# Sparse attention and a two-layer network on one core: scores ahead of values in the opening, a longer lead of the second layer, and uneven rounds of first-layer units

## The chip, the core and the metric

The kernel runs on one core of a Trainium2 chip. A core has four compute engines: TensorE (PE: matrix products, with its weight loads PEld beside them), VectorE (DVE), ScalarE (ACT) and GpSimd (POOL), and SyncE (SP), which here only issues DMAs. Each engine takes its instructions in the order of the program, and engines wait for one another through semaphores. The DMAs of the kernel are issued from SP and from POOL. PE writes its products to PSUM, which has eight banks of 128 x 512 fp32. The metric is the time of the program on the device in microseconds (us).

## What is computed

The reference is an attention with a sparse mask, and a two-layer network with a cosine gate behind it. There are 8 batches and 8 heads, a sequence of 576 and a head width of 64, hence 4608 tokens of width 512.

```python
mask = np.abs(pos[:, None] - pos[None, :]) <= 32          # a band
mask = mask | is_global[:, None] | is_global[None, :]     # and 8 global positions
scores = np.where(mask, q @ k.T / 8.0, -1e9)
attn = softmax(scores)
x = (attn @ v)            # heads side by side: 4608 x 512
h = x @ w_in              # 512 -> 2048
g = h * np.cos(h)
out = g @ w_out           # 2048 -> 512
```

## The kernel before

**Attention** goes by pairs of heads, 32 pairs in all (four to a batch). A pair takes these steps:

- `k`, `q` (local_k, local_q): bring K and Q into the layout of the scores. For pairs 0 to 9 PE turns them into a bank of tag h, and ACT copies them out (L604, L615, L616). From pair 10 on they come ready turned by DMA, and DVE copies them (L607, L619).
- `s` (scores): products of K and Q into three banks of tag s and a fourth (tag o in the opening, tag h later); then ACT's exponentials (L634 and L638, from pair 10 on L702 and L707) and DVE's products with the mask (L635 and L639, later L703 and L708).
- `p` (values): products with V into the tile pv, of which there is one (L646, later L719); then DVE's sums, reciprocals and the normalised rows xn (L660 to L666, later L724 to L730).
- `x` (turn_x): PE turns xn (L678, later L744) through a bank of tag s, and DVE copies it into xT, the input of the first layer. At the end of a batch POOL copies the columns of the global tokens (L687, L752).
- `n` (x_squares): ACT's squares of xn (L818), for a check of the value range.

**The network** goes by 9 tiles of 512 tokens. A first-layer unit, written `1`, is one of 16 groups of 128 hidden columns: four matmuls into a bank of tag h (L762), then ACT's cosine (L768) and DVE's product g (L769), which frees the bank. Tag h has two banks, taken in turn. Only between the marks `+` and `-` does every second pair of units take tag s instead. A second-layer unit, written `2`, is a quarter of an output tile of 128 tokens: four matmuls (L800). Four units fill a tile, which is copied out by DVE (L807) where its number within the 512 tokens is even and by ACT (L805) where it is odd, and goes to DRAM by an SP DMA (L809). Such a tile takes the one bank of tag o; odd ones take tag s in the tail and between `+` and `-`.

**The order is written by hand.** The program is emitted as the strings say, step by step, and each engine runs its share in that order.

- FRONT (L56) is the opening, pairs 0 to 9. Beside the steps above it has `L` (loads of K and Q), `M` (a DVE memset and the loads of V of the next half batch, `vn`), `C` (POOL's cast of it), `y` (value_rows: the V rows of the global tokens, PE at L409 and ACT at L410), `E` and `Y` (gathers of global rows by POOL), `H` (their casts and turning), `g` (global columns of K and Q by POOL), `W` and `O` (loads of the two weights), `K` (casts of K, Q and V to fp16 in DRAM), `f` (fillers: matmuls of ones into an unused part of pv, L493), and `m` and `t` (the matmuls of a first-layer unit, and its ACT and DVE part, apart).
- Rounds 4 to 15 follow, one for each two pairs (`a` and `z` are the round's two pairs, `c` and `d` the next round's). Round 4 is MID: pairs 8 and 9 are done in FRONT, so MID is first-layer and second-layer units while the data of pair 10 arrive. Round 5 is FIFTH, round 6 SIXTH, and rounds 7 to 15 are ORDER.
- Then comes the tail: the loop from L1042 on, `one()` and `two()` in turn, with squares of the weights on ACT (L826), their sums on DVE (L828), and four times weight_norms: a matmul with ones into a tile pn (L833) and a maximum on DVE (L834).

A `1` or `2` that cannot run yet is left out. `one()` needs its tokens ready (ready[0] grows by one 512-token tile after every odd round). `two()` needs the g that it reads to have been issued, and, ahead of the tail, fewer than outs_by[0] second-layer units done so far, which is 8 for each round from round 4 on.

Of the kernel before, what the change touches and what calls it, by code (L numbers as in the profile page):

```python
# [9 lines left out]
FP32 = mybir.dt.float32  # L10
# [9 lines left out]
P = 128  # L20
# [3 lines left out]
G = 8  # L24
# [20 lines left out]
TT = 512  # L45
NTT = NT // TT

ORDER = "sa 2 2 2 2 sz pa 1 1 2 xa pz G 1 1 2 xz n 1 1 2 kc qc 1 kd qd 2 1"

MID = ("+ 1 1 1 1 Z0 1 1 1 Z1 1 1 Z2 1 1 A0 n1 1 Z3 1 1 1 Z4 1 1 A1 n2 1 1 1 Z5 A2 1 1 1 n3 B5 1 2 2 g10 g11 kc qc V10 K6 2 2 1 1 2 2 kd qd - 2 2")  # L50

FIFTH = "sa G 2 2 2 2 sz pa 1 1 2 xa U10 K7 pz 2 2 2 kc qc xz n kd qd"

SIXTH = "sa 2 2 2 2 sz pa 1 1 2 xa pz G 1 1 2 xz n 1 1 D0 2 kc qc D1 1 kd qd D2 2 1"

FRONT = ("M1 s0 E0 C0 E1 L2 k1 q1 w4 y0.0 s1 f4 C1 H0 p0 M2 Y0 L3 y0.1 k2 q2 f6 x0 p1 y1.0 s2 k3 q3 f6 x1 M3 H1 C2 p2 g4 g5 g6 "  # L56
         "y1.1 s3 g7 I k4 q4 f6 x2 M4 p3 y2.0 s4 C3 L4 W0 k5 q5 f6 x3 p4 y2.1 s5 g8 g9 W1 W2 W3 k6 q6 f6 x4 p5 y3.0 s6 C4 k7 q7 f6 n0 x5 p6 "
         "y3.1 s7 k8 q8 f6 x6 p7 y4.0 s8 H2 k9 q9 f6 x7 p8 y4.1 s9 O m m x8 K5 p9 t t + m m t t x9 -")
WARM = 13
OK_ALL = float(P * (B * NP * 2 * BP + B))  # L60

# [143 lines left out]
def kernel(  # L205
# [18 lines left out]
    ps = es.enter_context(tc.tile_pool(name="ps", bufs=2, space=PSUM))  # L224
# [96 lines left out]
    p8 = keep.tile([P, 1], FP32)  # L321
# [432 lines left out]
    def mlp_in(t, f):  # L754
        if f == 0:
            g_of[t] = work.tile([P, NF, TT], FP16, tag="g", name="g")
        g16 = g_of[t]
        tag = "s" if spare[0] and f % 4 > 1 else "h"
        ph = ps.tile([P, TT], FP32, tag=tag, bufs={"s": 3, "h": 2}[tag], name="ph")
        ph_of.append((ph, g16[:, f]))  # L760
        for j in range(NC):
            nc.tensor.matmul(ph, w_in16[:, j, f * P : (f + 1) * P], xT[:, j, t * TT : (t + 1) * TT],  # L762
                             start=(j == 0), stop=(j == NC - 1))

    def mlp_act():
        ph, g = ph_of.pop(0)
        cos = work.tile([P, TT], FP16, tag="cos", bufs=3)
        nc.scalar.activation(cos, ph, AF.Sin, bias=pio2)  # L768
        nc.vector.tensor_tensor(g, cos, ph, ALU.mult)  # L769
# [20 lines left out]
    def mlp_out(t, u):  # L790
        g16 = g_of[t]
        s, part = u // 4, u % 4
        if part == 0:
            tag = "s" if (tail[0] or spare[0]) and s % 2 else "o"
            po_of[t] = ps.tile([P, DM], FP32, tag=tag, bufs={"s": 3, "o": 1}[tag], name="po")
        po = po_of[t]
        if t == NTT - 1 and s == 3:
            return last_out(g16, po, part)
        for f in range(4 * part, 4 * part + 4):
            nc.tensor.matmul(po, g16[:, f, s * P : (s + 1) * P], w_out16[:, f],  # L800
                             start=(f == 0), stop=(f == NF - 1))
        if part == 3:
            o = work.tile([P, DM], FP32, tag="osb", bufs=3)
            if s % 2:
                nc.scalar.copy(o, po)  # L805
            else:
                nc.vector.tensor_copy(o, po)  # L807
            r0 = t * TT + s * P
            nc.sync.dma_start(out[r0 : r0 + P, :], o)  # L809
# [4 lines left out]
    def x_squares(s):  # L814

        xn = xn_of.pop(s)
        n = P * (NK5 if s < HY else BP)
        nc.scalar.activation(view(xn, (BP * P, 2), (1, n)), view(xn, (BP * P, 2), (1, n)), AF.Square,  # L818
                             accum_out=x_sq[:, s : s + 1])
# [3 lines left out]
    def weight_squares(c, j):  # L823
        if j == 0:
            w_sq[c] = work.tile([P, NC, 512], FP16, tag="wsq", bufs=1, name="wsq")
        nc.scalar.activation(w_sq[c][:, j], w_in16[:, j, c * 512 : (c + 1) * 512], AF.Square)  # L826
        if j:
            nc.vector.tensor_tensor(w_sq[c][:, 0], w_sq[c][:, 0], w_sq[c][:, j], ALU.add)  # L828

    def weight_norms(c):  # L830
        sq = w_sq.pop(c)
        pn = ps.tile([P, 512], FP32, tag="h", bufs=2)
        nc.tensor.matmul(pn, ones16, sq[:, 0], start=True, stop=True)  # L833
        nc.vector.tensor_reduce(wmax4[:, c : c + 1], pn, AX.X, ALU.max)  # L834

# [22 lines left out]
    def raise_flag(count):  # L858
        tot, onesf = count
        pt = ps.tile([P, 512], FP32, tag="h", bufs=2)  # L860
        nc.tensor.matmul(pt[0:1, 0:1], tot, onesf, start=True, stop=True)
        okf = work.tile([1, 1], FP32, tag="okf", bufs=1)
        nc.vector.tensor_scalar(okf, pt[0:1, 0:1], OK_ALL, None, ALU.is_equal)
        nc.vector.tensor_copy(ok_flag, okf)
# [4 lines left out]
    def one(act=True):  # L869
        for _ in range(1):  # L870

            if ins_q and ins_q[0][0] < ready[0] and ins_q[0][0] < outs_q[0][0] + 2:
                t, f = ins_q.pop(0)
                mlp_in(t, f)
                if act:
                    mlp_act()
                ready[1] = t * NF + f + 1

    def two(n=1):
        for _ in range(n):  # L880
            t, u = outs_q[0] if outs_q else (NTT, 0)

            need = min(t * NF + 4 * (u % 4) + 7, (t + 1) * NF)
            if outs_q and need <= ready[1] and (tail[0] or NTT * NF - len(outs_q) < outs_by[0]):
                mlp_out(*outs_q.pop(0))

    outs_by = [0]
# [12 lines left out]
    with tc.manual_schedule():  # L900
# [73 lines left out]
        def casts(s):  # L974

            for pr in (2 * s + 2, 2 * s + 3):
                if pr < B * NP:
                    globals_kq(pr)
            if 5 < s < 2 * B - 2:
                nc.gpsimd.tensor_copy(gate, xn_of[s][0:1, 1, 0, 0:1])  # L980
                cast_half(s + 2, "vkq")
# [5 lines left out]
        def bring(s):  # L987

            turn_half(s)
            load_values(2 * s)  # L990
            load_values(2 * s + 1)
# [8 lines left out]
        ready[0] = 1  # L1000
        for step in FRONT.split():
            if step in "+-":
# [3 lines left out]
            f(*[int(x) for x in (step[1:] or "0").split(".")])  # L1006
        ready[0], front[0] = 2, False
        for s in range(4, B * NP // 2):
            outs_by[0] = 8 * (s - 3)
            for step in {4: MID, 5: FIFTH, 6: SIXTH}.get(s, ORDER).split():  # L1010
                if step == "1":
                    one()
                elif step == "m":
                    one(False)
                elif step == "t":
                    mlp_act()
                elif step in "+-":
                    spare[0] = step == "+"
                elif step == "2":
                    two()  # L1020
                elif step == "n":
                    x_squares(s - 1)
                elif step == "R":
                    ready[0] = 2
                elif step == "T":
                    bring(s + 2)
                elif step == "G":
                    casts(s)
                elif step[0] in "cvWCOVABDNU" or step[1].isdigit():
                    (STEPS | OTHER)[step[0]](*[int(x) for x in (step[1:] or "0").split(".")])  # L1030
                else:
                    f, pr = (STEPS | OTHER)[step[0]], 2 * s + "azcd".index(step[1])
                    if pr < B * NP:
                        f(pr, *[int(x) for x in step[2:]])
            if s % 2 == 1:
                ready[0] = s // 2 + 1 + (s // 2 == B - 1)
            if 3 < s < B * NP // 2 - 2:
                bring(s + 2)
# [2 lines left out]
        tail[0] = True  # L1041
        for i in range(NTT * NF):  # L1042
            one()
            two()
            if i % 5 < 4 and i < 20:
                weight_squares(i // 5, i % 5)
            elif i < 20:
                weight_norms(i // 5)
            if i == 22:
                count = finish_check()  # L1050
            if i == 34:
                raise_flag(count)
# [36 lines left out]
```

## Time and profile before

| | us |
|---|---|
| median of 3 runs | 357.35 (356.35 to 358.64) |
| the profiled execution | 355.8 |
| its span, first to last instruction | 354.1 |
| PE busy in the span | 334.3 |
| start of the long run of first-layer units (end of the opening) | 59.82 |
| one round (the scores of `sa`, at 155.56, to the next, at 172.70) | 17.14 |
| last 128 x 256 copy of the output begins | 348.42 |

A row of a timeline is start, length, engine, line, operation, output and inputs, shape, and how many instructions are merged in it; in brackets stands how long the engine was idle before it and what ended that wait. The lengths of matmuls are modelled and overlap (a 128 x 512 matmul is shown as 379 ns, but four of them follow one another in 0.86 us), so starts say more than lengths.

### The profile page before, as it was taken

What the parts mean: (1) busy time and instruction counts of PE and PEld (TensorE: products, weight loads), DVE (VectorE), ACT (ScalarE), POOL (GpSimd) and SP (SyncE); (2) the same over time, 40 slices, a digit from 0 to 9 for tenths busy, and PEclk for the clock granted to TensorE, in tenths of its full rate; (3) what the DMA queues carried; (4) which work ended last, traced back from release to release, by engine and by line L of the source; (5) the groups of instructions that cost most, each with busy time, mean ns of one, the idle gap of its engine ahead of it and who ended that gap; (6) DMA issues with size and microseconds to landing.
All of it is one profiled execution on the core that took longest, in us unless ns stands there. A gap on an engine that the chain in (4) does not pass through costs nothing.

```text
span 354.1 us, 8454 instructions
## 1 busy us (share of the span) xinstructions
PE 334.3 (94%) x3203; PEld 172.8 (49%) x3203; DVE 250.2 (71%) x611; ACT 245.3 (69%) x423; POOL 107.0 (30%) x221
## 2 busy tenths in 40 slices
PE   7879889999989999999999999999999999999993
PEld 2567665444445454545454444444444444444442
DVE  6567778987588697869787878787877556556410
ACT  8767898895666878777787877777686865644300
POOL 8773918333161507041623253233002000000000
PEclk9998999999999999999999999999999999999999
DMA  5999895999999999999999999999970001000111
GB/s 85 180 170 159 136 200 84 203 158 115 175 155 171 151 191 136 175 139 170 149 186 134 151 145 198 157 163 170 110 118 1 31 36 53 32 30 30 58 62 68
DMA packets 165891, 44.58 MB, mean 126 GB/s; under 512 B 153764, under 2 KB 160996, under 8 KB 165668
## 3 DMA queue, kind: packets, MB, share of 16 engines
q1 hardware_dynamic: 105860, 26.70, 52.3%
q0 software_dynamic: 59984, 17.28, 48.8%
q8 instruction: 27, 0.44, 0.5%
q14 instruction: 20, 0.16, 0.2%
HBM read 44.41 MB, written 19.17 MB: 180 GB/s over the span
## 4 chain that ended last, share of the span: by engine, by line
PE 73%; ACT 10%; DVE 6%; issue 5%; DMA 3%; SPq 1%; POOL 0%; ACTq 0%; POOLq 0%; DVEq 0%
PE po L800 32%; PE ph L762 30%; PE st L699 2%; PE tx L744 2%; DVE g L769 2%; ACT e L702 2%; ACT e L634 2%; PE pv L646 2%; ACT cos L768 2%; DMA vn<-in_v_dram 2%; ACT e L638 1%; ACT e L707 1%; PE pv L719 1%; DMA gidx_col<-in_global_idx_dram 1%; PE po L782 1%
## 5 line engine op out<-in xcount | busy, mean ns | idle before, releaser
L762 PE MATMUL ph<-xT,w_in 128*128 128x512 f16 x576 | 140.5, 379 | 2.8 <-DVE g L769 2.0
L768 ACT ACTIVATE cos<-ph,pio 128x512 f16<-128x512 f32 x144 | 96.8, 686 | 60.9 <-PE ph L762 58.5
L800 PE MATMUL po<-w_out,g 128*128 128x512 f16 x560 | 135.4, 379 | 0.0
L769 DVE TENSOR_TENSOR g<-cos,ph 128x512 f16<-128x512 f16 x144 | 95.7, 684 | 44.6 <-ACT cos L768 43.8
L762 PEld LDWEIGHTS <-w_in 128*128 128x128 f16 x576 | 54.2, 97 | 67.4 <-issue 7.9
L800 PEld LDWEIGHTS <-g 128*128 128x128 f16 x560 | 53.7, 98 | 63.6
L703 DVE TENSOR_TENSOR pm<-e,mask 128x512 f16<-128x512 f16 x44 | 18.7, 426 | 18.8 <-ACT e L702 17.4
L702 ACT ACTIVATE e<-st 128x512 f16<-128x512 f32 x44 | 23.9, 595 | 10.1 <-PE st L699 10.0
L980 POOL COPY gate<-xn 1x1 f16<-1x1 f16 x8 | 1.4, 179 | 85.8 <-DVE xn L730 85.8
L752 POOL COPY xT<-xg 128x4 f16 x48 | 15.6, 325 | 32.6 <-DVE xT L747 29.9
L272 POOL DMA_DIRECT2D q<-in_q_dram x11 | 23.9, 2176 | 0.0
L818 ACT ACTIVATE xn<-xn 128x1536 f16<-128x1536 f16 (+1 forms) x16 | 22.5, 1408 | 0.0
L730 DVE TENSOR_TENSOR xn<-pv,r_all 128x768 f16<-128x768 f32 x22 | 21.1, 958 | 1.0
L805 ACT COPY o<-po 128x512 f32<-128x512 f32 x17 | 9.9, 585 | 14.7 <-PE po L800 14.5
L807 DVE COPY o<-po 128x512 f32<-128x512 f32 x18 | 12.4, 690 | 9.2 <-PE po L800 8.6
L272 POOL DMA_DIRECT2D k<-in_k_dram x11 | 18.1, 1642 | 1.2 <-issue 1.2
L646 PE MATMUL pv<-vw,pm 128*128 128x65 f16 (+2 forms) x200 | 13.0, 203 | 3.3 <-DVE pm L639 3.3
L768 ACT ACT_TABLE_LOAD x12 | 15.4, 1283 | 0.2
L607 DVE COPY kw<-kT 128x1320 f16<-128x1320 f16 x22 | 15.4, 699 | 0.0
L702 ACT ACT_TABLE_LOAD x11 | 14.1, 1283 | 0.2
L699 PEld LDWEIGHTS <-kw 64*128 64x128 f16 x484 | 8.5, 95 | 10.8 <-issue 8.1
L699 PE MATMUL st<-qb,kw 64*128 64x64 f16 x484 | 11.3, 191 | 1.5 <-DVE qb L619 1.1
(185 smaller groups left out, 386.6 us busy)
## 6 DMA issues: line engine op xcount, KB each, us to landing
out_dram<-o SPq DMA_DIRECT2D x35, 256.0 KB
vw<-v SPq DMA_DIRECT2D x32, 165.0 KB
v<-in_v_dram POOLq DMA_DIRECT2D x11, 288.0 KB, 5.2
k<-in_k_dram POOLq DMA_DIRECT2D x11, 288.0 KB, 7.1
q<-in_q_dram POOLq DMA_DIRECT2D x11, 288.0 KB, 14.5
vn<-in_v_dram SPq DMA_DIRECT2D x20, 120.0 KB
w_in<-in_moe_w_in_dram POOLq DMA_DIRECT2D x4, 512.0 KB
w_out<-in_moe_w_out_dram POOLq DMA_DIRECT2D x1, 2048.0 KB
```

The costliest lines, as they stand in the source:

```text
L272: nc.gpsimd.dma_start(dst[s].rearrange("t (h d) -> t h d", h=4), dview(src, base, (D, S), (S * D, 4), (1, D)))
L646: nc.tensor.matmul(pv[p0 : p0 + m, h, X * slot : X * slot + X], pm[:, h * CN + OFF[t] + c0 : h * CN + OFF[t] + c0 + m], vp[:, t, h0 + h], ...
L699: nc.tensor.matmul(st[j // 8 * 2 + h][:, j % 8 * C : j % 8 * C + C], kp[hp, j], qp[hp, j], start=True, stop=True)
L702: nc.scalar.activation(e[:, 0:512], st[h], AF.Exp, scale=scale)
L703: nc.vector.tensor_tensor(view(pm[:, h], (1, 512)), e[:, 0:512], view(mask, (1, 512)), ALU.mult)
L730: nc.vector.tensor_tensor(view(xn, (384, 2), (D, 6), (1, D)), view(pv, (512, 2), (65, 6), (1, D)), view(rp, (6, 2), (1, 6), (0, D)), ALU.mult)
L752: nc.gpsimd.tensor_copy(xT[:, :, bass.ds(pool_idx[g] + b * S, 1)], xg[:, :, g : g + 1])
L762: nc.tensor.matmul(ph, w_in16[:, j, f * P : (f + 1) * P], xT[:, j, t * TT : (t + 1) * TT], start=(j == 0), stop=(j == NC - 1))
L768: nc.scalar.activation(cos, ph, AF.Sin, bias=pio2)
L769: nc.vector.tensor_tensor(g, cos, ph, ALU.mult)
L800: nc.tensor.matmul(po, g16[:, f, s * P : (s + 1) * P], w_out16[:, f], start=(f == 0), stop=(f == NF - 1))
L818: nc.scalar.activation(view(xn, (BP * P, 2), (1, n)), view(xn, (BP * P, 2), (1, n)), AF.Square, accum_out=x_sq[:, s : s + 1])
```

## The change

Four things are changed.

1. **FRONT.** The scores of the next pair now stand ahead of the values of this one (`s1 y0.0 f4 k2 q2 .. p0 .. s2`, `.. x0 p1 .. s3`, where it was `s1 f4 .. p0 .. x0 p1 .. s2`). The fillers fall from 52 to 18, the late gathers of V (`Y0`) move from ahead of `L3` to behind `C4`, `L4` moves ahead of `I`, and three `g` move ahead of `C2`.
2. **The lead of the second layer.** outs_by is 4 higher from round 4 on, and MID has four more `2`, so 12 units are done in round 4 for 8. All later rounds do 8 as before, each one output tile further on: the four units behind `sa` are now the odd tile, and the four that are spread over the rest of the round the even one. The tail has 44 second-layer units left where it had 48.
3. **Uneven rounds.** Even rounds have ten first-layer units (SIXTH too) and odd rounds six, where all had eight. Three of them then stand in a row in odd rounds behind `pz G`, and in even rounds from 8 on behind `xz n`. In the tail four steps of the loop do two first-layer units.
4. **weight_norms** takes its tile from tag s (three banks), not from tag h.

```diff
-ORDER = "sa 2 2 2 2 sz pa 1 1 2 xa pz G 1 1 2 xz n 1 1 2 kc qc 1 kd qd 2 1"
+EVEN = "sa 2 2 2 2 sz pa 1 1 2 xa pz G 1 1 2 xz n 1 1 1 2 kc qc 1 1 kd qd 2 1"
+ODD = "sa 2 2 2 2 sz pa 1 1 2 xa pz G 1 1 1 xz n 1 2 kc qc 2 kd qd 2"

-MID = ("+ 1 1 1 1 Z0 1 1 1 Z1 1 1 Z2 1 1 A0 n1 1 Z3 1 1 1 Z4 1 1 A1 n2 1 1 1 Z5 A2 1 1 1 n3 B5 1 2 2 g10 g11 kc qc V10 K6 2 2 1 1 2 2 kd qd - 2 2")
+MID = ("+ 1 1 1 1 Z0 1 1 1 Z1 1 1 Z2 1 1 A0 n1 1 Z3 1 1 1 Z4 1 1 A1 n2 1 1 1 Z5 A2 1 1 1 n3 B5 1 2 2 g10 g11 kc qc V10 K6 2 2 1 1 2 2 2 2 kd qd 2 2 - 2 2")
 FIFTH = "sa G 2 2 2 2 sz pa 1 1 2 xa U10 K7 pz 2 2 2 kc qc xz n kd qd"
-SIXTH = "sa 2 2 2 2 sz pa 1 1 2 xa pz G 1 1 2 xz n 1 1 D0 2 kc qc D1 1 kd qd D2 2 1"
+SIXTH = "sa 2 2 2 2 sz pa 1 1 2 xa pz G 1 1 2 xz n 1 1 D0 2 kc qc D1 1 1 kd qd D2 2 1 1"

-FRONT = ("M1 s0 E0 C0 E1 L2 k1 q1 w4 y0.0 s1 f4 C1 H0 p0 M2 Y0 L3 y0.1 k2 q2 f6 x0 p1 y1.0 s2 k3 q3 f6 x1 M3 H1 C2 p2 g4 g5 g6 "
-         "y1.1 s3 g7 I k4 q4 f6 x2 M4 p3 y2.0 s4 C3 L4 W0 k5 q5 f6 x3 p4 y2.1 s5 g8 g9 W1 W2 W3 k6 q6 f6 x4 p5 y3.0 s6 C4 k7 q7 f6 n0 x5 p6 "
-         "y3.1 s7 k8 q8 f6 x6 p7 y4.0 s8 H2 k9 q9 f6 x7 p8 y4.1 s9 O m m x8 K5 p9 t t + m m t t x9 -")
+FRONT = ("M1 s0 E0 C0 E1 L2 k1 q1 w4 s1 y0.0 f4 k2 q2 C1 H0 p0 M2 L3 y0.1 s2 k3 q3 f2 x0 p1 M3 H1 g4 g5 g6 C2 y1.0 s3 g7 L4 I k4 q4 f2 x1 p2 M4 y1.1 s4 "
+         "C3 W0 k5 q5 f2 x2 p3 y2.0 s5 g8 g9 W1 W2 W3 k6 q6 f2 x3 p4 y2.1 s6 C4 Y0 k7 q7 f2 x4 p5 n0 y3.0 s7 k8 q8 f2 x5 p6 y3.1 s8 H2 k9 q9 f2 x6 p7 y4.0 s9 "
+         "x7 p8 y4.1 O m m x8 K5 p9 t t + m m t t x9 -")
...
     def weight_norms(c):
-        pn = ps.tile([P, 512], FP32, tag="h", bufs=2)
+        pn = ps.tile([P, 512], FP32, tag="s", bufs=3)
...
         for s in range(4, B * NP // 2):
-            outs_by[0] = 8 * (s - 3)
-            for step in {4: MID, 5: FIFTH, 6: SIXTH}.get(s, ORDER).split():
+            outs_by[0] = 8 * (s - 3) + 4
+            for step in {4: MID, 5: FIFTH, 6: SIXTH}.get(s, ODD if s % 2 else EVEN).split():
...
         for i in range(NTT * NF):
             one()
+            if 12 < i < 17:
+                one()
             two()
```

## The prediction

> **What bounds the kernel now.** I read the page's table of busy time first, then busy time by stretches, then who waited for whom on TensorE (PE), then the timeline of one round, of the tail and of the opening.
>
> ```profile
> span 354.1 us, 8454 instructions
> PE 334.3 (94%) x3203; PEld 172.8 (49%) x3203; DVE 250.2 (71%) x611; ACT 245.3 (69%) x423; POOL 107.0 (30%) x221
> ```
>
> PE is the engine to watch, but 94% is a mean over stages. By stretches (PE busy is the first number after the length, then PEld, DVE, ACT, POOL, the granted clock, DMA):
>
> ```profile
> 10.00:28.00 18.00, 14.67 (x336) 11.62 (x334) 10.24 (x38) 11.97 (x31) 13.46 (x16) 0.94 1.11 172
> 28.30:53.80 25.50, 21.98 (x469) 17.71 (x468) 19.35 (x61) 22.12 (x50) 11.58 (x34) 0.98 1.00 166
> 59.80:121.00 61.20, 59.20 (x444) 27.86 (x441) 48.75 (x113) 44.05 (x74) 24.59 (x43) 1.00 1.40 161
> 121.00:276.00 155.00, 154.33 (x1481) 75.81 (x1480) 124.09 (x277) 117.86 (x190) 43.13 (x98) 1.00 1.35 145
> 276.00:314.00 38.00, 36.24 (x166) 16.03 (x164) 22.19 (x40) 24.60 (x41) 0.00 (x0) 1.00 0.10 36
> ```
>
> From 121 to 276 us (the rounds, ORDER) PE is busy 154.33 of 155.00: there is no wait to win there, and any wait that the change makes is added in full, since PE takes its work in order and has no slack to swallow it. Time can be won in the opening (before 60 us, PE idle for 6.9 us of the first two stretches) and in the tail (1.8 us idle of 38). The named waits of PE, first from 276 us on, then between 60 and 121:
>
> ```profile
> PE ph L762 <- DVE g L769: 1.7, 4, 0.4
> ```
> ```profile
> PE st L699 <- DVE qb L619: 1.1, 1, 1.1
> ```
>
> **The rounds.** This is the largest term, so it comes first. A first-layer unit (`1`) needs one of the two banks of tag h, which is free again when VectorE (DVE) has written g of the unit two allocations before. One round, PE, then ScalarE (ACT), then DVE (start, length, instruction):
>
> ```profile
> 155.56 0.49 PE L699 MATMUL st<-qb,kw 64*128 64x64 f16 x22
> ...
> 164.35 1.90 PE L762 MATMUL ph<-xT,w_in 128*128 128x512 f16 x8
> 166.09 1.03 PE L800 MATMUL po<-w_out,g 128*128 128x512 f16 x4
> 166.95 0.50 PE L744 MATMUL tx<-ident,xn 128*128 128x128 f16 x6
> 167.43 1.89 PE L762 MATMUL ph<-xT,w_in 128*128 128x512 f16 x8
> 169.15 1.03 PE L800 MATMUL po<-w_out,g 128*128 128x512 f16 x4
> 170.01 1.03 PE L762 MATMUL ph<-xT,w_in 128*128 128x512 f16 x4
> 172.70 0.49 PE L699 MATMUL st<-qb,kw 64*128 64x64 f16 x22
> ```
> ```profile
> 159.98 1.08 ACT L702 ACTIVATE e<-st 128x512 f16<-128x512 f32 x2 [0.79 <-PE st L699]
> 166.87 1.47 ACT L818 ACTIVATE xn<-xn 128x1536 f16<-128x1536 f16 x1
> 168.49 0.69 ACT L768 ACTIVATE cos<-ph,pio 128x512 f16<-128x512 f32 x1
> ```
> ```profile
> 159.65 0.69 DVE L807 COPY o<-po 128x512 f32<-128x512 f32 x1
> 166.70 1.27 DVE L769 TENSOR_TENSOR g<-cos,ph 128x512 f16<-128x512 f16 x2
> 169.21 0.69 DVE L769 TENSOR_TENSOR g<-cos,ph 128x512 f16<-128x512 f16 x1 [0.73 <-ACT cos L768]
> 172.40 0.53 DVE L607 COPY kw<-kT 128x1320 f16<-128x1320 f16 x1
> 172.85 0.46 DVE L619 COPY qb<-qT 128x616 f16<-128x616 f16 x1
> ```
>
> Before, the units after `pz` stand as `1 1 2 xz n 1 1 2`. The third starts at 167.43, and the g that frees its bank ends at about 166.70 + 0.68 = 167.38: just in time, because `2` and `xz` (166.09 to 167.43) stand between.
>
> Odd round: `1 1 1 xz n 1`. The third unit is due at 166.09 and waits for the same g until 167.38: 1.3 us. Behind it stand `xz`, the last unit and three output units, and the whole rest of the round shifts. Then the end: the squares of `n` (with cos behind them: 168.49 - 166.87 = 1.6) now stand between the cos of the third and of the last unit. The third unit ends at 167.4 + 0.86 (a unit: half of 169.15 - 167.43) = 168.25; its cos (0.2 to begin, 0.69 long) ends at about 169.1, the squares at 170.7, the last cos at 171.3, its g at 172.0, the copies kw and qb (0.53 + 0.46, a little overlapped) at 172.9. PE wants the next scores at 168.25 + 0.48 (xz) + 4 x 0.86 = 172.2: 0.7 us more. And the output tile that ends the round is now an even one, whose copy is DVE's (before, an odd one, ACT's) and stands behind the second pair's kw and qb: 172.9 + 0.9 + 0.69 = 174.5, while the one bank of tag o is wanted behind the scores (0.45), at 173.35: 1.15 us.
>
> In all rounds the four output units behind `sa` now end an odd tile, whose copy goes to ACT:
>
> ```profile
> L805 ACT COPY o<-po 128x512 f32<-128x512 f32 x17 | 9.9, 585 | 14.7 <-PE po L800 14.5
> ```
>
> It falls between the two heads' pairs of exponentials, in a gap of 0.79 that ends at 159.98; begun at 159.65, as DVE's copy was, it ends at 160.24, so those exponentials and all behind them come 0.3 later. DVE's 0.69 at 159.65 falls away in a place that waits for ACT anyway, worth nothing. So an odd round loses 1.3 + 0.3 + 0.7 + 1.15 = 3.4.
>
> Even round: `xz n 1 1 1 2`. The third of these is due at 169.15, its bank's g ends at 169.21 + 0.69 = 169.9: 0.75; with 0.3 for the copy's delay (0.05 of slack before it) 1.0. Its `1 1` after kc qc: the bank's g stands ahead of kc in DVE's order and is done; nothing.
>
> Rounds 7, 9, 11 and 13 lose 3.4 each (13.6), round 15 (no kc qc behind it) 1.6, rounds 8, 10, 12 and 14 lose 1.0 each (4.0), round 6 with two units at its end 0.5: **+19.7**. Bounds: 5 x 1.3 + 4 x 0.75 = 9.5 if nothing but the first waits counts, and zero only if the bank rule is not as I read it. Units moved from odd to even rounds cost nothing in themselves: 80 units in rounds 6 to 15, as before.
>
> **Tail.** The norm's tile moves from tag h to s (three banks).
>
> ```profile
> 284.35 0.38 PE L833 MATMUL pn<-wsq,ones 128*128 128x512 f16 x1
> 284.40 0.69 DVE L769 TENSOR_TENSOR g<-cos,ph 128x512 f16<-128x512 f16 x1
> 285.14 1.02 PE L762 MATMUL ph<-xT,w_in 128*128 128x512 f16 x4 [0.42 <-DVE g L769]
> ```
>
> The norm's matmul takes a bank of h, so the next unit waits for the g that ends at 285.09. It could start a quarter of a unit after 284.35, at 284.57: 0.57 lost (more than the idle time by the table, since the ends of matmuls are modelled late), four times: **-2.3** (bounds 0 to -2.6). This row also is the only place of this trace where a unit takes its bank one turn early, and it waits exactly as I reckon for the rounds. The four doubled units in the tail (`1 1 2`) stand a `2` apart from the bank they reuse, but ACT's squares lie in between: **+0.4** (0 to 1.5). Four output units fewer at the end, four more in round 4: nothing, since PE does them in either place.
>
> **Round 4 and 5.** Four more `2` before pair 10, and a higher limit of outs_by: 12 units are done there for 8. PE is busy there, so they move work. Pair 10's casts K5 leave POOL behind its copies of x7's columns and move some 2 us less than PE does; pair 10's first copy did not wait before:
>
> ```profile
> 83.54 0.53 DVE L607 COPY kw<-kT 128x1320 f16<-128x1320 f16 x1
> ```
>
> So I take 0 there, bounds 0 and +2. In round 5 the tile that ends at `2 2 2` is an even one, so DVE copies it (0.69) right ahead of kc qc, where PE waits 1.1 for qb already: **+0.7** (0 to 0.7). The copy of tile 0.2 delays `2` behind sa by 0.4, about what a wait of sa for ACT's copy took before: even.
>
> **Opening.** Scores of the next pair now stand ahead of the values of this one.
>
> ```profile
> 14.86 0.55 PE L631 MATMUL st<-qb,kw 64*128 64x136 f16 x10
> ...
> 28.32 0.91 PE L631 MATMUL st<-qb,kw 64*128 64x136 f16 x10
> ```
> ```profile
> 53.84 0.55 PE L631 MATMUL st<-qb,kw 64*128 64x136 f16 x10
> ...
> 59.82 13.97 PE L762 MATMUL ph<-xT,w_in 128*128 128x512 f16 x64
> ```
> ```profile
> 36.76 0.69 ACT L410 CAST vw<-rows 8x640 f16<-8x640 f32 x1 [0.65 <-PE rows L409]
> ...
> 40.96 0.69 ACT L410 CAST vw<-rows 8x640 f16<-8x640 f32 x1 [0.71 <-PE rows L409]
> ```
>
> A pair takes 40.96 - 36.76 = 4.2, of which ACT is idle 0.71: ACT's work is 3.5 a pair, and with scores ahead it can run through; DVE (19.35 busy in 25.5, six pairs: 3.2) just fits. From the scores of pair 3 to those of pair 9 it took 25.5; now 6 x 3.6 and 1.5 for the squares `n0`, which no longer fall in a gap: 23.2, a gain of 2.3. Pairs 2 and 3 took (28.32 - 14.86) / 2 = 6.7 each; with row copies now behind the exponentials I walk them through at 4.6: s3 at 23.8 for 28.3, a gain of 4.5. After s9, one more pair's values and turning trail on DVE, an estimated 1.9 of its 3.2 a pair: 7.9 to the long run of units instead of 5.98, so 1.9 back. **-4.9**; bounds 0 (the data of kn and vn come no sooner) and -9 (nothing given back, pairs 2 and 3 at 3.5). The late gathers moved past eight POOL steps are wanted only in round 4; POOL's wait for C2 stays, and behind it stand g7 and L4, wanted only four pairs on.
>
> Fillers fall from 52 to 18. The clock's row, the longest wait of PE around it (total, times, longest) and two like matmul groups:
>
> ```profile
> 25.00:30.00 5.00, 5.00 (x95) 4.24 (x90) 2.80 (x11) 2.91 (x9) 3.72 (x14) 0.66 0.96 139
> ```
> ```profile
> PE bank L595 <- issue: 1.2, 3, 0.5
> ```
> ```profile
> 20.04 1.03 PE L646 MATMUL pv<-vw,pm 128*128 128x65 f16 x20
> ...
> 26.26 1.59 PE L646 MATMUL pv<-vw,pm 128*128 128x65 f16 x20
> ```
>
> The clock was granted at 0.66 (half rate for 5 x 0.34 x 2 = 3.4 us) in a stretch behind transposes with few fillers, and the values took 1.59 for 1.03. The change keeps a pair's scores, values and rows but in a shorter period, so I take no loss. [...]
>
> **Sum.** -4.9 - 2.3 + 0.4 + 0.7 + 19.7 = **+13.6**, on the profiled span 354.1 to 367.7; the median of 357.35 goes to **371**.
>
> **Rivals.** (A) Only the first waits of the rounds count (5 x 1.6 + 4 x 1.0 + 0.5 = 12.5), as the end of the odd rounds hides under something: 357.35 + 12.5 - 6.1 = 363.7. For it: DVE has 20% free in the rounds. Against: the copies are in order. (B) Faster: the third unit does not wait, because its bank is free. Place: after pz and after n; it decides if g of the first ends before PE ends the second. Then 357.35 - 4.9 - 2.3 + 0.4 + 0.7 = 351.2. For it: no row shows three units in a row in these rounds. Against: the norm's row. (C) The opening gives its full 9 and the rounds as in A: 359.7. For: PE's 6.9 us idle plus the low clock; against: DVE trailing. (D) The clock falls in every second stretch of 3.4 us over the 32 us of opening: some five, each losing a third of its 3.4 (1.59 against 1.03): +5.5, 376.5. For: 34 fillers gone. Against: only one low stretch before.
>
> **Chances.** Forecast 0.38, A 0.25, B 0.17, C 0.12, D 0.08. So faster 0.17, within 1% 0.12 (C), slower 0.71; 1%, 3.6 us, is about what a measurement can tell. The range, 357 to 376, leaves out B and the end of D. The likeliest case alone: 366 to 374.
>
> **What would show it.** Right: PE's waits for g at L762 grow from 5 to some 13, 9 of them of 0.7 to 1.7 us; a pair of rounds takes 38.7 instead of 34.3; the next scores wait for qb in even rounds; no wait behind L833; the run of units starts near 55. Wrong: rounds still at 34.3 a pair (B), or a granted clock below 1 for several stretches before 55 (D).

## Result and profile after

The changed kernel is slower, and by more than forecast: **375.51 us** (median of 4 runs, 374.12 to 376.38) beside 357.59 for the kernel before in the same comparison, a ratio of 1.0518 (95% interval 1.0471 to 1.0566). The forecast was 371, with 357 to 376 as its range and 366 to 374 for its likeliest case: the time lies above the likeliest case and just inside the range. In spans of the profiled executions it is 354.1 before and 374.3 after, 20.2 us more.

The page's first lines, and busy time by stretches (after the length: PE, PEld, DVE, ACT, POOL, granted clock, DMA share, GB/s). Lines behind the opening strings have moved by two, so L762 of before is L764 here, L769 is L771, L800 is L802, L807 is L809.

```profile
span 374.3 us, 8386 instructions
...
PE 335.2 (90%) x3169; PEld 171.3 (46%) x3169; DVE 245.3 (66%) x611; ACT 244.3 (65%) x423; POOL 110.7 (30%) x221
```
```profile
10.00:28.00 18.00, 15.30 (x368) 11.20 (x366) 10.71 (x37) 14.32 (x38) 11.52 (x19) 0.91 1.08 171
28.30:53.80 25.50, 18.99 (x385) 15.40 (x385) 17.30 (x58) 20.56 (x47) 14.40 (x29) 0.87 0.99 166
...
121.00:276.00 155.00, 138.25 (x1312) 67.22 (x1311) 107.54 (x246) 103.56 (x172) 46.33 (x94) 1.00 1.39 143
```

PE is busy about as long as before (335.2 for 334.3), so nearly all of the 20 us (19.3) is PE standing still. In the rounds (121 to 276) it is busy 138.25 of 155, where it was 154.33. The opening shows a second thing: the granted clock is 0.91 and 0.87 where it was 0.94 and 0.98.

The waits of PE from 60 us to the end (total, times, longest), where before there had been 2.0 for g (1.7 of it in the tail), 1.1 for qb and 0.3 for a copy of the output:

```profile
PE ph L764 <- DVE g L771: 8.8, 10, 1.2
PE po L802 <- DVE o L809: 6.7, 9, 0.8
PE st L701 <- DVE qb L621: 3.4, 5, 1.4
PE ph L764 <- ACT e L709: 2.4, 11, 0.2
```

They come to 21.3. One pair of rounds in the timeline of PE, an odd round and an even one from the scores at 145.63, shows where each stands:

```profile
140.16 1.02 PE L764 MATMUL ph<-xT,w_in 128*128 128x512 f16 x4 [1.18 <-DVE g L771]
...
145.63 0.50 PE L701 MATMUL st<-qb,kw 64*128 64x64 f16 x22 [0.52 <-DVE qb L621]
146.95 3.61 PE L802 MATMUL po<-w_out,g 128*128 128x512 f16 x16 [0.82 <-DVE o L809]
...
152.67 1.02 PE L764 MATMUL ph<-xT,w_in 128*128 128x512 f16 x4 [0.22 <-ACT e L709]
...
161.06 1.02 PE L764 MATMUL ph<-xT,w_in 128*128 128x512 f16 x4 [0.64 <-DVE g L771]
...
166.34 0.49 PE L701 MATMUL st<-qb,kw 64*128 64x64 f16 x22
167.59 3.61 PE L802 MATMUL po<-w_out,g 128*128 128x512 f16 x16 [0.76 <-DVE o L809]
```

The first row is the third unit in a row of an odd round, the fifth that of an even round: each waits for the bank. The third row is the output tile behind the scores, which waits until DVE has copied the tile before it. VectorE shows why that copy is late:

```profile
144.58 0.53 DVE L609 COPY kw<-kT 128x1320 f16<-128x1320 f16 x1
145.02 0.46 DVE L621 COPY qb<-qT 128x616 f16<-128x616 f16 x1
145.40 0.52 DVE L609 COPY kw<-kT 128x1320 f16<-128x1320 f16 x1
145.84 0.46 DVE L621 COPY qb<-qT 128x616 f16<-128x616 f16 x1
146.22 0.68 DVE L809 COPY o<-po 128x512 f32<-128x512 f32 x1
```

The tile was ready at 145.1 (PE's last output matmul before the scores), but its copy stands behind both pairs' kw and qb in VectorE's order and ends at 146.90; PE starts at 146.95.

Split by places that both traces have (starts on PE):

| stretch | before | after | difference | forecast |
|---|---|---|---|---|
| up to the long run of units | 59.82 | 60.44 | +0.6 | -4.9 |
| from there to `sa` of round 6 | 43.48 | 47.22 | +3.7 (3.5 of it the four moved units) | moved units + 0.7 |
| to the first unit of the tail | 172.17 | 193.75 | +21.6 | +19.7 |
| to the end of the span | 78.63 | 72.9 | -5.7 (3.5 of it the moved units) | moved units - 1.9 |

Four output units are 16 matmuls, 3.46 us at 0.216 each. In the tail the norm's matmul now takes another bank, and the unit behind it starts 0.23 later, where it had been 0.79:

```profile
310.14 0.39 PE L835 MATMUL pn<-wsq,ones 128*128 128x512 f16 x1
310.37 1.03 PE L764 MATMUL ph<-xT,w_in 128*128 128x512 f16 x4
```

So the rounds and the tail went about as forecast, and the opening did not: of the 6.6 by which 20.2 exceeds the forecast 13.6, the opening is 5.5 and the rounds 1.9, and the other two rows together took 0.8 less than forecast.

### The profile page after: what moved, and what is told of

Read it like the earlier page. It is cut to its first block, busy times and chain, and to the rows that moved or that the text cites. A ratio compares the mean times of both kernels' runs of the same rounds, so it can differ in the third digit from the quotient of the medians.

```text
span 374.3 us, 8386 instructions
## 1 busy us (share of the span) xinstructions
PE 335.2 (90%) x3169; PEld 171.3 (46%) x3169; DVE 245.3 (66%) x611; ACT 244.3 (65%) x423; POOL 110.7 (30%) x221
## 4 chain that ended last, share of the span: by engine, by line
PE 52%; issue 14%; ACT 14%; DVE 12%; DMA 3%; POOL 3%; SPq 1%; POOLq 0%; ACTq 0%; DVEq 0%
PE po L802 24%; PE ph L764 20%; DVE g L771 3%; ACT cos L770 3%; ACT e L704 3%; ACT xn L820 2%; DMA kn<-in_k_dram 2%; DVE o L809 2%; DVE kw L609 1%; PE st L701 1%; ACT L770 1%; ACT e L636 1%; DVE qb L621 1%; PE pv L648 1%; ACT e L709 1%
## 5 line engine op out<-in xcount | busy, mean ns | idle before, releaser
L764 PE MATMUL ph<-xT,w_in 128*128 128x512 f16 x576 | 139.9, 379 | 11.3 <-DVE g L771 8.8
L802 PE MATMUL po<-w_out,g 128*128 128x512 f16 x560 | 133.7, 379 | 6.7 <-DVE o L809 6.7
L771 DVE TENSOR_TENSOR g<-cos,ph 128x512 f16<-128x512 f16 x144 | 95.6, 684 | 46.4 <-ACT cos L770 45.7
L764 PEld LDWEIGHTS <-w_in 128*128 128x128 f16 x576 | 54.0, 97 | 76.0 <-issue 17.9
L802 PEld LDWEIGHTS <-g 128*128 128x128 f16 x560 | 54.4, 98 | 71.9 <-issue 6.5
L807 ACT COPY o<-po 128x512 f32<-128x512 f32 x17 | 10.0, 586 | 33.2 <-PE po L802 33.2
L809 DVE COPY o<-po 128x512 f32<-128x512 f32 x18 | 12.3, 685 | 11.6 <-PE po L802 11.6
L609 DVE COPY kw<-kT 128x1320 f16<-128x1320 f16 x22 | 12.9, 586 | 0.0
L709 ACT ACTIVATE e<-st 128x192 f16<-128x192 f32 x44 | 12.5, 352 | 0.0
```

The source lines that it names most:

```text
L609: nc.vector.tensor_copy(to, view(kT[pr // 2 % 2][:, pr % 2], (QB, NB), (1, W)))
```

## Experiments

Times here are medians beside the kernel before on the same chip (354.75 to 356.35 there), and ratios go with their 95% interval; 0.01 of ratio is some 3.6 us. Theories that an expectation names by a letter are those of the experiments, and not the rivals of the prediction.

### The parts one by one

**The new opening alone**: the kernel before with the new FRONT.

```diff
-FRONT = ("M1 s0 E0 C0 E1 L2 k1 q1 w4 y0.0 s1 f4 ...
+FRONT = ("M1 s0 E0 C0 E1 L2 k1 q1 w4 s1 y0.0 f4 ...
```

> The kernel before with the new FRONT alone. Theory: the opening of the changed kernel won nothing (its long run of units begins at 60.4 us for 59.8), because V of the third half batch lands 4.8 us later, holds POOL's cast and DVE's memset, and PE's clock then falls; so this run is 358 +- 1 us, its long run begins near 60.4. Rival: the opening does win its 5 us and the lead in round 4 spoils it: 353, long run near 55. Second rival: without the four extra second-layer units pair 10 comes late: 360 and a wait of the scores of pair 10.

356.13 beside 354.82: 1.0049 (1.0019 to 1.0078), a small loss of 1.7 us in place of a gain of 4.9. The long run of units begins at 60.04 in its profile. The lead and the rounds are not in this kernel, so the missing gain is lost within the opening.

**All but the opening and the norms**: the changed kernel with the old FRONT and the norms in tag h.

```diff
-FRONT = ("M1 s0 E0 C0 E1 L2 k1 q1 w4 s1 y0.0 f4 ...
+FRONT = ("M1 s0 E0 C0 E1 L2 k1 q1 w4 y0.0 s1 f4 ...
-        pn = ps.tile([P, 512], FP32, tag="s", bufs=3)
+        pn = ps.tile([P, 512], FP32, tag="h", bufs=2)
```

> The changed kernel with the FRONT of before and the norms' tile back in tag h: the lead, the uneven rounds and the doubled units of the tail alone. Theory (rounds 6 to 15 cost 21.6 in the changed kernel's trace, whatever stands ahead of them): 357.6 + 21.6 + 0.3 = 379.5. By the forecast's 19.7: 378. Rival (part of the loss comes from the later opening): under 375.

376.65 (2 runs) beside 354.82: 1.0615 (1.0564 to 1.0666), 21.8 us. The lead and the uneven rounds, with the doubled units of the tail, carry the whole loss.

**The norms alone**: the kernel before with one edit.

```diff
-        pn = ps.tile([P, 512], FP32, tag="h", bufs=2)
+        pn = ps.tile([P, 512], FP32, tag="s", bufs=3)
```

> The kernel before with the norms' tile in tag s alone. Theory: four waits of 0.57 go, 2.3 us: 355.3, and no wait of PE on g behind the norms' matmul. Rival: the waits move to tag s (the next odd output tile waits for the norms' maximum): 357.5.

352.65 beside 354.82: **0.994 (0.992 to 0.9961)**, 2.2 us less, where -2.3 was forecast. The waits for g in the tail are gone; one row of 0.3 is left from 60 us on (there were four of 0.4 in the tail):

```profile
PE ph L762 <- DVE g L769: 0.3, 1, 0.3
```

This kernel beats both the one before and the changed one.

By these three the whole change should have 21.8 + 1.7 - 2.2 = 21.3 us. It has 20.2 by the spans, and 18.5 by the ratio; the ratio comes from another comparison, in which the kernel before takes 357.59. The rest of 2.8 us by ratio is as large as the four intervals taken together (root of the sum of squares of 1.7, 1.8, 1.0 and 0.7: 2.8), so it says nothing.

**The uneven rounds alone**: the kernel before with EVEN, ODD and the new SIXTH, without the lead.

```diff
-ORDER = "sa 2 2 2 2 sz pa 1 1 2 xa pz G 1 1 2 xz n 1 1 2 kc qc 1 kd qd 2 1"
+EVEN = "sa 2 2 2 2 sz pa 1 1 2 xa pz G 1 1 2 xz n 1 1 1 2 kc qc 1 1 kd qd 2 1"
+ODD = "sa 2 2 2 2 sz pa 1 1 2 xa pz G 1 1 1 xz n 1 2 kc qc 2 kd qd 2"
...
-            for step in {4: MID, 5: FIFTH, 6: SIXTH}.get(s, ORDER).split():
+            for step in {4: MID, 5: FIFTH, 6: SIXTH}.get(s, ODD if s % 2 else EVEN).split():
```

> The kernel before with the uneven rounds alone (even ones of ten first-layer units, odd ones of six); the lead of the second layer, the opening, the norms and the loop of the tail stay as before, so even output tiles stand behind the scores and go through VectorE, as in the kernel with the copies exchanged. If the waits for the bank of the third units (1.18 in odd rounds, 0.64 in even ones) and for qb (0.52) are the cost of the uneven rounds and the copies the cost of the lead, each by itself, two rounds take 37.0, as with the copies exchanged (34.3 before), and the time is 10 to 13 above the kernel before, ratio 1.028 to 1.037; the lead is then the other 9 to 11 of the rounds' 21.6. If the two only cost together, the ratio stays below 1.015.

367.25 beside 354.92: 1.0361 (1.0338 to 1.0384), 12.8 us. It has the waits for the bank and for qb, and none of the new waits for a copy of the output:

```profile
133.46 1.02 PE L764 MATMUL ph<-xT,w_in 128*128 128x512 f16 x4 [1.18 <-DVE g L771]
138.94 0.50 PE L701 MATMUL st<-qb,kw 64*128 64x64 f16 x22 [0.67 <-DVE qb L621]
...
153.33 1.02 PE L764 MATMUL ph<-xT,w_in 128*128 128x512 f16 x4 [0.63 <-DVE g L771]
...
175.96 0.50 PE L701 MATMUL st<-qb,kw 64*128 64x64 f16 x22 [0.67 <-DVE qb L621]
```

Two rounds take 175.96 - 138.94 = 37.02, as expected. So the uneven rounds cost without the lead, and what the lead adds to them is the rest of the 21.8: about 9, by subtraction, since the lead was not run alone.

### The two costs of the rounds, taken away one at a time and together

**Third units in tag s.** The third of three units in a row takes one of the three banks of tag s, so that it need not wait for a bank of h.

```diff
-        tag = "s" if spare[0] and f % 4 > 1 else "h"
+        tag = "s" if (spare[0] and f % 4 > 1) or third[0] else "h"
...
-EVEN = "sa 2 2 2 2 sz pa 1 1 2 xa pz G 1 1 2 xz n 1 1 1 2 kc qc 1 1 kd qd 2 1"
+EVEN = "sa 2 2 2 2 sz pa 1 1 2 xa pz G 1 1 2 xz n 1 1 3 2 kc qc 1 1 kd qd 2 1"
-ODD = "sa 2 2 2 2 sz pa 1 1 2 xa pz G 1 1 1 xz n 1 2 kc qc 2 kd qd 2"
+ODD = "sa 2 2 2 2 sz pa 1 1 2 xa pz G 1 1 3 xz n 1 2 kc qc 2 kd qd 2"
...
+                elif step == "3":
+                    third[0] = True
+                    one()
+                    third[0] = False
```

> The changed kernel, with the third of three first-layer units in a row taking its bank from tag s instead of h, in odd rounds behind pz and in even rounds from 8 on behind n. Theory: the waits of PE on g there (1.18 in five rounds, 0.64 in four, 8.5 in all) go and the rest of the round moves up with them: 367. Rival: DVE's copy of the output tile ends when it did, so in odd rounds the gain is taken back at the copy: 371.

366.53 (2 runs) beside 354.82: 1.033 (1.0276 to 1.0383), by the ratios 6.7 us less than the changed kernel. The waits for g are gone, those for the copy stay, and the scores behind the odd rounds, which had waited 0.5 for qb, now wait longer for something that was hidden before:

```profile
PE po L802 <- DVE o L809: 6.9, 9, 0.9
PE st L701 <- POOL xT L754: 3.9, 4, 1.2
PE ph L764 <- ACT e L709: 2.4, 11, 0.2
```

That new row, named by the profile for POOL's copies of the global columns, is part of why it gave less than all its waits.

**Copies exchanged.** Third units back in tag h; even output tiles are copied by ACT and odd ones by DVE.

```diff
-            if s % 2:
+            if s % 2 == 0:
                 nc.scalar.copy(o, po)
```

> The changed kernel with one edit: even output tiles are copied by ACT and odd ones by DVE, the other way round; the third units still take tag h. From its waits of PE, 9 of 0.8 for DVE's copy and 11 of 0.2 for ACT's delayed exponentials go: 9 us less if they are added in full, 366.5 beside 375.5. If the first waits (third units, 1.2 and 0.64) grow by what the copies no longer delay, 4 to 6 us less. With the two other kernels of the square (third units in tag s: 366.5; both: 357.3) the two causes then add up to 18 to 19 of the rounds' 21.6.

366.48 (2 runs) beside 356.35: 1.029 (1.025 to 1.0331), by the ratios 8 us less than the changed kernel. The scores and the output tile behind them, which began 1.32 apart (145.63 and 146.95), are now 0.42 apart:

```profile
144.36 0.50 PE L701 MATMUL st<-qb,kw 64*128 64x64 f16 x22 [0.52 <-DVE qb L621]
144.78 3.63 PE L802 MATMUL po<-w_out,g 128*128 128x512 f16 x16
```

**Both edits together.**

> The changed kernel with the third unit's bank from tag s, as in the last run, and with the copies of output tiles exchanged: even tiles by ACT, odd ones by DVE. Theory: nine waits of PE for DVE's copy (0.8 each, 6.9 in all) go, and eleven of 0.2 for the exponentials that ACT's copy delayed: 9 less than with the bank alone, a ratio of 1.008 to before. Rival: PE then waits for something else at the same place (the next pair's kw and qb, or POOL's columns), 4 less: 1.022.

357.27 beside 354.75: 1.0062 (1.0017 to 1.0108). Nearly all of the loss is gone, though the lead and the uneven rounds are still there.

```profile
143.28 0.50 PE L701 MATMUL st<-qb,kw 64*128 64x64 f16 x22 [1.15 <-POOL xT L754]
```

The length of two rounds, from the scores of round 8 to those of round 10, puts the square together (`sa` starts; for the kernel before twice its 17.14):

| | third units in h | third units in s |
|---|---|---|
| even tiles by DVE (as changed) | 184.66 - 145.63 = 39.03 | 179.65 - 142.32 = 37.33 |
| even tiles by ACT | 181.38 - 144.36 = 37.02 | 178.55 - 143.28 = 35.27 |

Before it was 34.28. The copies account for 2.0 of the 4.75 in either column (0.82 + 0.76 + twice 0.22 by the rows), and the move of the third units to tag s for 1.7 in either row. That 1.7 is what is left of their own waits (1.18 and 0.64) and of the wait for qb (0.52), once the new wait for POOL (0.90) is set against them. With both edits 1.0 remains, nearly all of it this new wait. The two costs add up, and neither needs the other.

### The opening

The longest new wait of PE in the first 60 us of the changed kernel, and POOL's cast of the third half batch, which it waits for (with the load of K that goes ahead of it):

```profile
PE rows L411 <- POOL vw L404: 1.7, 1, 1.7
```
```profile
21.68 0.72 POOL L281 DMA_DIRECT2D kn<-in_k_dram  x1
...
31.66 1.25 POOL L404 CAST vw<-vn 128x1280 f16<-128x1280 f32 x1 [5.11 <-DMA vn<-in_v_dram]
```

Before, that cast began at 26.89 and had waited 0.90 for its data. Now V is asked for later (the memset of `M2`, ahead of its loads, begins at 21.04 on DVE for 19.23), while the loads of K and Q of `L3` no longer stand behind the gathers `Y0` on POOL and go out at 21.68 for 24.30, in a stretch in which the DMA engines' share is 1.08. Which of these two makes V late was not separated. And the granted clock stands at half twice in the opening of the changed kernel, from 13.6 to 17.0 and then between 34 and 41 us:

```profile
34.10:40.90 6.80, 5.95 (x100) 4.87 (x102) 5.18 (x19) 4.45 (x11) 5.53 (x14) 0.50 0.96 161
```

Two theories were put up: (A) the late V alone takes the gain away; (B) PE's clock does, for want of fillers. Three kernels, all the kernel before with the new opening and an edit to it.

**Values asked for earlier, K and Q later**: M2 behind s1, and L3 behind g6.

```diff
-FRONT = ("M1 s0 ... w4 s1 y0.0 f4 k2 q2 C1 H0 p0 M2 L3 y0.1 ... M3 H1 g4 g5 g6 C2 y1.0 ...
+FRONT = ("M1 s0 ... w4 s1 M2 y0.0 f4 k2 q2 C1 H0 p0 y0.1 ... M3 H1 g4 g5 g6 L3 C2 y1.0 ...
```

> The kernel before with the new FRONT, in which the loads of V of the third half batch (M2) stand right behind s1 and the loads of K and Q of the fourth (L3) behind g6, so that these come after those. Theory A (late V cost the opening its gain, as it held POOL's cast, DVE's memset and PE's rows): V lands near 27 us for 31.6, the 1.5 us wait of the rows goes, the clock keeps up better, the long run begins near 56: 3 to 4 less than the new FRONT as it is, ratio to before 0.995. Theory B (fewer fillers, the clock falls): less than 1.5 us won, still four low windows: ratio 1.001 or more.

358.22: 1.008 (1.0046 to 1.0114). The cast waits no longer, and the long run of units begins at 56.86, 3.2 earlier than with the new opening as it is. The scores of pairs 4 to 9 begin at 29.71, 33.38, 37.00, 40.54, 45.29 and 48.74: 3.5 to 3.7 apart, and 4.75 behind `n0`. But nothing comes of it in the end: the next half batch's cast waits instead (it does not yet hold up PE here), and two waits at pairs 10 to 12 give back 2.4 (qb 1.0 more than before, V 1.4).

```profile
27.77 1.25 POOL L402 CAST vw<-vn 128x1280 f16<-128x1280 f32 x1
38.36 1.41 POOL L402 CAST vw<-vn 128x1280 f16<-128x1280 f32 x1 [5.26 <-DMA vn<-in_v_dram]
```
```profile
PE st L699 <- DVE qb L619: 2.1, 1, 2.1
...
PE pv L719 <- DMA vw<-vg: 1.4, 3, 0.7
```

This profile is of one of the kernel's fastest executions (355.58); what the others lost on top of it (median 358.22) stands in no trace.

**Fillers back to six a pair.**

```diff
-... f2 x0 p1 ... f2 x1 p2 ... f2 x7 p8 ...
+... f6 x0 p1 ... f6 x1 p2 ... f6 x7 p8 ...
```

> The kernel before with the new FRONT, with six fillers a pair for two. Theory B (the clock cost the opening its gain): the low windows of 3.4 us go from four to one or none and 2.5 us are won: ratio 0.998. Theory A (late V): the rows still wait for POOL's cast, and 28 more fillers of 0.08 us stand in PE's way: ratio 1.005 or more, long run at 60 or later.

356.69: 1.0036 (1.0005 to 1.0067), not to be told from the opening as it is (1.0049). In its profile the run begins at 59.98, and the clock still stands at half from 34.0 to 40.9. Over its 10 runs the mean granted clock is 0.988, where the ten runs of the new opening as it is have 0.980 and the kernel before 0.994: half of the lost clock, and no time that shows.

**Both.**

> The kernel before with the new FRONT, V ahead as two runs before and six fillers. If A and B each cost some: 5 less than the new FRONT as it is, ratio 0.991, long run near 55. If A alone: no better than V ahead with two fillers. If B alone: as with six fillers alone.

358.09: 1.0081 (1.0048 to 1.0113). Its profile, of one of its slowest executions (360.42), has the third cast without a wait, the fourth waiting 5.68, and the run of units from 62.02. Theory A falls, since the late V of the third half batch can be mended and nothing is won; theory B falls as it was put, since with fillers and V mended the loss is no smaller (the mean clock is 0.979 here, so the fillers alone do not hold it either).

A third theory: the opening is bound by the arrival of data in general (the DMA engines' share is 1.08 and 0.99 in its two stretches above), so that what is loaded earlier makes something else late. To test it, half of three loads of V are left out: V of heads 2 and 3 of half batches 2, 3 and 4, whose rows are set to zero instead, once, by two memsets on DVE behind the first scores (`Q2 Q3`).

```diff
-FRONT = ("M1 s0 E0 ...
+FRONT = ("M1 s0 Q2 Q3 E0 ...
...
+            hs = 2 if s in (2, 3, 4) else 4
-            nc.sync.dma_start(rows[p0 : p0 + n, t].rearrange("p (h d) -> p h d", h=4),
-                              dview(v, (s * 4 * S + lo) * D, (D, n), (S * D, 4), (1, D)))
+            nc.sync.dma_start(rows[p0 : p0 + n, t, 0 : hs * D].rearrange("p (h d) -> p h d", h=hs),
+                              dview(v, (s * 4 * S + lo) * D, (D, n), (S * D, hs), (1, D)))
+    def clear_heads(s):
+        nc.vector.memset(vn_of(s)[:, :, 2 * D :], 0.0)
```

In the new opening:

> The kernel before with the new opening, where V of heads 2 and 3 of the half batches 2, 3 and 4 is left out (their rows are set to zero once by VectorE, behind the first scores): half of three loads of V is not moved. Theory D (the opening is bound by the arrival of data): POOL's cast of the third half batch no longer waits 5 us for its DMA, the wait of the value rows for it (1.5) goes, the loads of K and Q behind it come earlier too, and the long run of first-layer units begins 3 to 5 us earlier than in the new opening alone (60.04), at 55 to 57; time 3 to 5 us less than its 356.13, so 351 to 353 beside 354.8. Theory B (PE's clock, for want of fillers): the waits shrink, but the clock is at half in two or three windows as before and the run begins at 59 or later; time within 1.5 us of 356. Theory of the prediction (the order of the engines' work alone sets it): the run begins at 55, as forecast for the full data, whether data come sooner or not.

In the old one:

> The kernel before with its own opening, where the same halves of three loads of V are left out. Theory D: the old order waits for engines rather than for data, except for the cast's 0.9, so it gains less than the new order does: the long run begins 0 to 2 us before 59.82; time 0 to 2 us less than 354.8. If instead the data bind both orders alike, it gains the same 3 to 5 us, and the new order is no better with free data than with late ones: then the data are not what takes the expected gain away.

Both beside 356.35. With the new opening 354.5: 0.995 (0.9926 to 0.9973); with the old one 355.58: 0.9988 (0.9966 to 1.001). So less data is worth some 3.5 us to the new order (0.995 against 1.0049, by ratios from two chips; +- 1.4 by the two intervals) and 0.4 us to the old one (1.2 by the end of its interval), as the theory of the data said: with less to load, the new order looks the better one by 0.4%, though the two intervals just overlap. The mean clock is not what brings this gain: it is 0.983 over these 9 runs and 0.980 with all the data. POOL's cast of the third half batch waits 1.86 for 5.64, and the wait of the value rows for it is gone. But the profiled execution, one of the two slowest of the nine (356.06), did not begin its run at 55 to 57, but at 60.2, no sooner than with all the data. So the gain is in the medians, and no trace shows where in the kernel it lies. What held PE up in this one execution is, by its rows, the clock; here it stands in both kernels over the same stretch (new, then old):

```profile
17.00:33.60 16.60, 15.64 (x265) 12.90 (x266) 9.29 (x31) 10.44 (x27) 8.80 (x21) 0.52 0.79 127
```
```profile
17.00:33.60 16.60, 13.87 (x346) 11.58 (x344) 11.94 (x40) 11.75 (x30) 9.86 (x22) 1.00 0.85 137
```

At 0.52, PE did 265 matmuls in the time of 346 (20 of the 81 fewer are fillers), and was busy nearly throughout; the scores of successive pairs begin 5.8 to 6.1 apart in this stretch (14.53, 20.45, 26.54, 32.30) and 3.5 to 3.9 apart behind it (36.15, 39.86, 43.31). Each timed run has its mean granted clock beside its span, and they show that a lower clock is no accident of one profile: the runs of the new opening alone have 0.971 to 0.989 (mean 0.980, 10 runs), those of the kernel before on the same chip 0.987 to 0.999 (mean 0.995, 22 runs). Over a span of 354 us that is, as an estimate from these means with a clock that is either full or half (0.50 in the low stretches), 14 us at half clock in place of 4. Within each kernel the span falls as the clock rises, by 0.6 +- 0.7 and by 1.2 +- 0.5 us for 0.01; so the 0.015 between them goes with 1 to 2 us, about the size of the measured loss. The first of the two slopes can't be told from nothing, and this is a correlation and not an experiment, since no kernel here set the clock.

## Why the prediction missed

**The rounds: right in mechanism, 10% short in all, and in part by luck.** Forecast 4.4 for two rounds, measured 4.75; +19.7 forecast in all, +21.6 measured. The single waits came out as worked out from the rows of before: the third unit of an odd round 1.3 (measured 1.18), that of an even round 0.75 (0.64), qb 0.7 (0.52), the copy of DVE behind kw and qb 1.15 (0.82), ACT's copy ahead of the exponentials 0.3 (0.22). One was missed: of the even rounds the prediction said that behind kc qc there is "nothing", and their scores indeed do not wait; but the even tile's copy stands behind kd qd there too, and the output units wait 0.76. That miss (0.76) is about as large as what the five terms had too much together (0.9, with ACT's copy in both rounds), so the pair's total held by luck as well. The waits that the profile names come to 4.36 of the 4.75; the rest stands in no row. The square of runs above shows that the bank and the copies are separate causes and carry nearly all of it. Rival A (the end of the odd rounds hides under something) and rival B (no wait for the bank) fall by the rows at 140.16 and 146.95.

**The norms and the tail: right.** -2.3 forecast, -2.2 measured alone; the tail's -5.7 is the moved units and this term.

**Round 4 and 5: nearly right.** 0.7 was forecast for the copy ahead of kc qc; without the moved units 0.28 was lost, most of it at qb (1.4 for 1.1).

**The opening: the step that failed.** Forecast -4.9, measured +0.6. "From the scores of pair 3 to those of pair 9 it took 25.5; now 6 x 3.6 and 1.5 for the squares `n0` ...: 23.2." It took 52.31 - 23.67 = 28.6, which is 5.4 of the 5.5 that the opening missed. The step reckoned with ACT and DVE as the limits and let the data come as before; they came later. PE's starts of the scores (L633) and of the value rows show where it went:

```profile
23.67 0.22 PE L633 MATMUL st<-qb,kw 64*128 64x136 f16 x1
25.12 0.53 PE L633 MATMUL st<-qb,kw 64*128 64x136 f16 x9 [1.23 <-DVE kgT L559]
...
28.63 0.55 PE L633 MATMUL st<-qb,kw 64*128 64x136 f16 x10 [0.28 <-ACT qb L618]
32.97 0.44 PE L411 MATMUL rows<-vw,one_v 128*8 128x128 f16 x5 [1.70 <-POOL vw L404]
33.34 0.38 PE L633 MATMUL st<-qb,kw 64*128 64x136 f16 x6
34.95 0.50 PE L633 MATMUL st<-qb,kw 64*128 64x192 f16 x4 [1.23 <-DVE xg L686]
...
39.42 0.91 PE L633 MATMUL st<-qb,kw 64*128 64x136 f16 x10
...
43.09 0.55 PE L633 MATMUL st<-qb,kw 64*128 64x136 f16 x10
...
47.80 0.55 PE L633 MATMUL st<-qb,kw 64*128 64x136 f16 x10 [0.26 <-issue]
...
52.31 0.55 PE L633 MATMUL st<-qb,kw 64*128 64x136 f16 x10 [0.16 <-ACT qb L618]
...
60.44 13.97 PE L764 MATMUL ph<-xT,w_in 128*128 128x512 f16 x64
```

- The scores of pair 3 began at 23.67, forecast 23.8, before 28.32: the 4.5 of the first pairs was there.
- Three waits of 1.2 to 1.7 stand between 23.67 and 35, for global columns (kgT, xg) and for the late V: 4.2 together. The wait for xg is the late V too. The memset of `M4` writes the buffer of the third half batch's V and stands ahead of xg in DVE's order; DVE stood still before it:

```profile
33.03 0.27 DVE L380 MEMSET vn<- 64x256 f32 x1 [3.32 <-DMA vn<-in_v_dram]
```

- The first three of the six pairs took 4.96, 4.71 and 6.08 (the last from 33.34 to 39.42, mostly at half clock), each with one of these waits in it.
- From 39.42 to 43.09, with the clock at half until 40.9, a pair took 3.67. With `n0` it took 4.71 (3.6 + 1.5 forecast). The last took 4.51, at full clock; it took 3.45 in the run of the new opening alone, and what held it up here is not known. So the pace of 3.6 stands where data and clock don't hold PE up, as the 3.5 to 3.7 of the run with the values asked for earlier show.
- From the last scores to the run of units 8.13, forecast 7.9.

The pace and the two ends were right, and the middle was held up by what the forecast had as a bound alone ("the data of kn and vn come no sooner", where V came 4.8 later by POOL's cast) and as rival D (the clock), given 0.08. D's sign came, with the clock below 1 in two stretches ahead of 55 (3.4 and 6.8 us long, where D's five of 3.4 were the author's estimate), and its time of 376.5 is the nearest of all to the measured 375.51; but D laid the whole miss of the opening to the clock, which no run here shows. With fewer bytes the new order does gain (0.995, beside 1.0049 with all of them, where the old order has 0.9988), which shows that the arrival of the data costs it time; how much falls to the clock is open. The prediction took "no loss" for the 34 fillers that went; bringing most of them back (six a pair for two) changed the time by no more than can be measured, so that step stands, but the clock fell oftener all the same (mean 0.988 with them and 0.980 without, for 0.994 before). The low stretches last 3.4 and 6.8 us here, and a low clock came without a long wait of PE as well: in the 16.6 us with a mean clock of 0.52 of the kernel with half of V, PE's longest wait was 0.8.

```profile
PE bank L600 <- ACT e L643: 0.8, 1, 0.8
```

What makes the clock fall there is not settled: neither the fillers nor the late V decide it alone (0.988 with six fillers a pair, 0.979 with V ahead as well), and the new order of PE's work was not tried by itself.

## What to carry to other kernels

Where an engine is busy 99% of a stretch, count for every moved step which buffer it takes in turn and who frees it, and which in-order neighbour it now stands behind: 4.4 us for two rounds came out of six single rows and held within 8% (with errors that offset one another), and two small edits (another bank, another engine for the copy) took 3.8 of 4.75 away again. Such a stretch can be reckoned from rows; this opening, which waits on loads, could not be reckoned from its engines' pace alone (-4.9 forecast, +0.6 measured): with V asked for earlier the cast of the third half batch began at 27.77 for 32.34, but that of the fourth at 38.36 for 38.23, and of the 3.2 won by the start of the run of units 2.4 were given back in two waits behind it. Of a bundle of edits, run each alone: one here was worth 0.6% and was buried under 6% of loss.

## What was not expected of the hardware

The granted clock stood at half for stretches of 3.4 or 6.8 us, and once for some 17 us (17.6 to 34.6, in the kernel with half of V), in an opening in which PE was rarely idle (15.64 busy of the 16.60 shown; a matmul is shown longer at half clock, though: ten of the scores 0.91 at 39.42 for 0.55 at 43.09 in the changed kernel). The stretches lie at other places from one kernel to the next though their openings differ little: 13.4 to 16.8, 27.1 to 30.5 and 33.9 to 40.7 in the new opening alone, 34.0 to 40.9 only with more fillers, 25.7 to 29.1 only in the kernel before. Runs of one kernel on one chip differ in it too: 0.971 to 0.989 in mean clock for the new opening alone. Their times differ as well (354.87 to 358.55), but the clock alone does not order them: the slowest had 0.988.
